# Three more products in the first down-projection round: eight plain block products in place of seven, and a new order of all work

## The chip, the cores and the metric

One core of one Trainium2 chip. The metric is the device time of one execution in microseconds (us), lower is better. The core has five engines that run side by side, each through its own list of instructions: PE multiplies matrices into PSUM, DVE (vector), ACT (scalar) and POOL (GpSimd) work elementwise, SP issues the DMA transfers.

## The reference, cut to what matters

```python
kv = einsum('bhsd,bhse->bhde', k, v); out = einsum('bhsd,bhde->bhse', q, kv)   # 4 x 8 heads, 576 tokens, 64
x = out / sqrt(mean(out*out, -1) + 1e-6) * g_norm       # -> x: 2304 tokens x 512
x = ((x @ w_a) * (x @ w_b)) @ w_out                     # first block, d_ff = 1536
return (sigmoid(x @ w_gate) * (x @ w_val)) @ w_out2     # second block, the same sizes
```

All of it is float32.

## The kernel before, in words

**Tiling.** The two blocks (m = 0, 1) are cut into six rounds each (q = 0 to 5); a round takes 256 of the 1536 middle columns (two weight chunks, u and v, of 128). In each round the 2304 tokens go in three groups (j = 0, 1, 2) of 768, each in two halves of 384. A group is named (m, q, j), and there are 36. Every matrix product is done by a Strassen scheme: the operands are cut into 2 x 2 blocks and seven block products replace eight, at the cost of sums and differences of blocks on the elementwise engines. A float32 operand is split into a high part, made by an ACT copy, and a low part, which is the source less the high part, made by DVE or POOL (h and l in names, lines 951 and 954 for activations, 536 and 540 for weights); a block product is three passes (high x high, high x low, low x high).

**A group's up-projection.** Seven products with u and v parts, 14 steps named `("P", g, i, "u" or "v")`, each of 6 matmuls of 384 columns (line 842). Then lines 899 to 919 form the product a*b: `gf1` (second half of the tokens) after products 5 and 4, `gf0` (first half) after product 3.

**A group's down-projection.** Seven products `("down", g, i)`, i from DOWNS = "1265734", each 6 matmuls (line 997). Their left operands are `G1` (the parts of `gf1`), and `S12`, `G22` and `S34`, which are the parts of sums of blocks made at line 934 (`s12g`, `s34g`). Their weights are four tiles `wo0` to `wo3`: `wo0` and half-tile `wo3` are parts of the weights, `wo1` and `wo2` are parts of block differences (`tmp`, line 520). Product 1 is common to two outputs: it opens PSUM pair 0, and `seed` (line 1004, ACT) copies it to pair 1. Pair 0 is held from product 1 to product 4. Results go into `part`: the first sum of an output block in round q = 0 is a plain copy (lines 447 and 449), all others are DVE additions (line 1026). So in round q = 0 a group has four copies and two additions.

**Weights.** They come as 64-bit words and are decoded on ACT, DVE and POOL (lines 475 to 497) into `w32`, then split by `w_parts` (line 512).

**What sets the order.** `Plan.order` (line 191) runs a list scheduler over all operations before the kernel is emitted: each has a cost, the operations it comes after, and a due time worked back from those that need it; an engine that comes free takes the ready operation with the least due time. `SHIFT` (line 57) adds a number of ns to the due time of a named operation: a positive one makes it less urgent. PSUM is four pairs of banks; pairs are given out strictly in the order in which the operations were created (line 259). Operations with `port=True` on DVE and POOL are never planned at the same time. The slots of line 41 say where the seven downs of the group before stand between the 14 product steps.

**Before the rounds.** The attention stage (lines 646 to 797) makes x in eighteen token tiles; its last tiles are still in work while the first two groups' products run. `x_comb` (line 553) makes the block sums of x of each group in round 0 (lines 567, 586, 589).

Of the kernel before, what the change touches and what calls it, by code (L numbers as in the profile page):

```python
# [46 lines left out]
DOWNS = "1265734"  # L47

# [17 lines left out]
    ('t13', 'wp', 1, 1): 170030, ('shift', (0, 'o')): 48280, ('clamp', (1, 'o')): 196670,  # L66
    ('t24', 'wo', (0, 0), 0): 67470, ('t13', 'wo', (0, 0), 1): 117760, ('wo0', (0, 0), 'l'): 59440,
# [16 lines left out]
    ('shift', (16, 'b')): 3400, ('t13', 'wp', 16, 0): 78700, ('wp0', 16, 'h'): 84360, ('wp3', 16, 'l'): 168520,
    ('t24', 'wp', 17, 1): -77400, ('clamp', (17, 'o')): 61540, ('wo3', (1, 2), 'h'): 70860, ('mag', (19, 'b')): 22720,
    ('w32', (19, 'b')): 35820, ('t13', 'wp', 18, 1): 5650, ('wo3', (1, 3), 'h'): 71380, ('load', (21, 'a')): -44050,
    ('shift', (21, 'a')): -34340, ('sign', (21, 'a')): -33010, ('last', (21, 'b')): 115060,
    ('t13', 'wp', 20, 0): 78700, ('wp2', 20, 'l'): 9920, ('t24', 'wp', 21, 0): -51740, ('t24', 'wp', 21, 1): -77490,
    ('mag', (21, 'o')): 180540, ('last', (22, 'b')): -23780, ('load', (23, 'a')): -49000, ('w32', (23, 'a')): -5650,
    ('t13', 'wp', 22, 0): 78700, ('wp2', 22, 'l'): 9920, ('t13', 'wp', 23, 0): -38040, ('xl', (0, 0, 0), '2'): 4130,  # L90
    ('xs', (0, 0, 0), '3'): -396300, ('P', (0, 0, 0), '2', 'u'): -414200, ('P', (0, 0, 0), '2', 'v'): -305030,
    ((0, 0, 0), 'c11'): 107780, ('P', (0, 0, 0), '7', 'v'): -29380, ('P', (0, 0, 0), '5', 'u'): 117720,
    ('P', (0, 0, 0), '5', 'v'): 49410, ((0, 0, 0), 'S12', 'l'): 186710, ((0, 0, 0), 'G22', 'h'): 162310,
    ((0, 0, 0), 'S34', 'l'): 92600, ('xh', (0, 0, 1), '2'): 42800, ('xl', (0, 0, 1), '2'): 119180,
    ('xh', (0, 0, 1), '7'): 269090, ('xh', (0, 0, 1), '4'): 21020, ('xl', (0, 0, 1), '4'): 27490,
    ('P', (0, 0, 1), '1', 'u'): 73740, ('P', (0, 0, 1), '1', 'v'): 88930, ('seed', (0, 0, 0)): 75880,
    ('P', (0, 0, 1), '5', 'u'): 98290, ((0, 0, 1), 'G22', 'l'): 39170, ((0, 0, 1), 'S34', 'h'): -72980,
    ('xs', (0, 0, 2), '5'): 154010, ('xl', (0, 0, 2), '7'): 15840, ('xl', (0, 0, 2), '4'): 30900,
    ('xs', (0, 0, 2), '3'): 335000, ('xl', (0, 0, 2), '3'): 98720, ('xd', (0, 0, 2), '3'): 332700,
    ('down', (0, 0, 1), '1'): 24410, ('P', (0, 0, 2), '2', 'u'): -128360, ('P', (0, 0, 2), '2', 'v'): 105070,  # L100
    ('down', (0, 0, 1), '5'): 19000, ('P', (0, 0, 2), '5', 'v'): 128990, ('P', (0, 0, 2), '4', 'v'): 28600,
    ((0, 0, 2), 'G1', 'l'): 163880, ((0, 0, 2), 'S34', 'h'): 74750, ('xh', (0, 1, 0), '6'): 60660,
    ('xh', (0, 1, 0), '3'): 193920, ('down', (0, 0, 2), '7'): 92580, ('sum', (0, 0, 2), '7'): 15470,
    ((0, 1, 0), 'S34', 'h'): -27040, ('down', (0, 1, 0), '2'): -197540, ('P', (0, 1, 1), '2', 'u'): -28400,
    ('down', (0, 1, 0), '6'): -86130, ('P', (0, 1, 1), '7', 'u'): -51550, ('down', (0, 1, 0), '5'): -33610,
    ('down', (0, 1, 0), '7'): -158610, ('down', (0, 1, 0), '3'): 20750, ('P', (0, 1, 1), '3', 'u'): 17430,
    ('P', (0, 1, 1), '3', 'v'): 139830, ('P', (0, 1, 2), '1', 'open'): 173480, ('P', (0, 1, 2), '2', 'v'): 5780,
    ('sum', (0, 1, 1), '5'): 31510, ('P', (0, 1, 2), '5', 'v'): -86130, ('P', (0, 2, 0), '5', 'open'): 13280,
    ('P', (0, 2, 0), '4', 'u'): 63490, ('P', (0, 2, 0), '4', 'v'): 144740, ('P', (0, 2, 1), '6', 'v'): -125580,
    ('P', (0, 2, 1), '2', 'v'): 17500, ('sum', (0, 2, 0), '5'): 24550, ('P', (0, 2, 1), '4', 'u'): 16740,  # L110
    ('P', (0, 2, 1), '4', 'v'): 8560, ('down', (0, 2, 0), '4'): 14790, ('P', (0, 2, 1), '3', 'u'): 17430,
    ('P', (0, 2, 1), '3', 'v'): 139830, ('P', (0, 2, 2), '1', 'open'): 139930, ('P', (0, 2, 2), '2', 'v'): 5780,
    ('P', (0, 2, 2), '5', 'v'): -86130, ('sum', (0, 2, 2), '6'): 186670, ('down', (0, 2, 2), '3'): 200070,
    ('P', (0, 3, 0), '4', 'v'): 144740, ('P', (0, 3, 1), '6', 'u'): -94550, ('P', (0, 3, 1), '6', 'v'): -125580,
    ('down', (0, 3, 0), '2'): -204820, ('P', (0, 3, 1), '2', 'u'): -28400, ('P', (0, 3, 1), '2', 'v'): 17500,
    ('P', (0, 3, 1), '5', 'u'): -60900, ('P', (0, 3, 1), '4', 'u'): 16740, ('P', (0, 3, 1), '4', 'v'): 8560,
    ('down', (0, 3, 0), '4'): 14790, ('P', (0, 3, 1), '3', 'u'): 17430, ('P', (0, 3, 1), '3', 'v'): 139830,
    ('P', (0, 3, 2), '1', 'open'): 139930, ('P', (0, 3, 2), '5', 'v'): -86130, ('P', (0, 3, 2), '3', 'u'): 1010,
    ('P', (0, 3, 2), '3', 'v'): -320, ('P', (0, 4, 0), '5', 'open'): 13280, ('down', (0, 3, 2), '3'): 200070,
    ('P', (0, 4, 0), '4', 'u'): 63490, ('P', (0, 4, 0), '4', 'v'): 144740, ('P', (0, 4, 1), '6', 'v'): -125580,  # L120
    ('P', (0, 4, 1), '2', 'v'): 17500, ('P', (0, 4, 1), '5', 'u'): -60900, ('P', (0, 4, 1), '5', 'v'): -27020,
    ('P', (0, 4, 1), '4', 'u'): 16740, ('P', (0, 4, 1), '4', 'v'): 8560, ('down', (0, 4, 0), '4'): 14790,
    ('P', (0, 4, 1), '3', 'u'): 17430, ('P', (0, 4, 1), '3', 'v'): 139830, ('P', (0, 4, 2), '3', 'u'): 1010,
    ('P', (0, 4, 2), '3', 'v'): -320, ('P', (0, 5, 0), '5', 'open'): 13280, ('down', (0, 4, 2), '3'): 200070,
    ('P', (0, 5, 0), '4', 'u'): 63490, ('P', (0, 5, 0), '4', 'v'): 144740, ('down', (0, 5, 0), '2'): -204820,
    ('P', (0, 5, 1), '2', 'v'): 17500, ('P', (0, 5, 1), '4', 'u'): 16740, ('P', (0, 5, 1), '4', 'v'): 8560,
    ('down', (0, 5, 0), '4'): 14790, ('P', (0, 5, 1), '3', 'u'): 17720, ('P', (0, 5, 1), '3', 'v'): 139070,
    ('P', (0, 5, 2), '1', 'open'): 140220, ('down', (0, 5, 2), '3'): 200070, ('sum', (0, 5, 2), '3'): 37620,
    ('xl', (1, 0, 2), '7'): -34020, ('xh', (1, 1, 0), '3'): 213490, ((1, 1, 0), 'c11'): -175520,
    ('P', (1, 1, 0), '5', 'u'): 123560, ((1, 1, 0), 'G1', 'l'): 39790, ((1, 1, 0), 'S34', 'h'): 35780,  # L130
    ('P', (1, 1, 1), '1', 'open'): 198010, ('P', (1, 1, 1), '7', 'u'): -21180, ((1, 1, 1), 'gf1'): 75540,
# [1006 lines left out]
```

## Time and profile before

| | us |
|---|---|
| median of 3 runs (lowest to highest) | 908.66 (908.51 to 909.37) |
| the profiled execution | 905.58 |
| its span, first to last instruction | 903.6 |
| PE busy | 861.3 (95%) |
| DVE busy | 728.9 (81%) |
| POOL busy | 476.7 (53%) |
| ACT busy | 463.5 (51%) |

The span is what the trace covers; the execution is 1.98 us longer. Busy shares are means over stages that differ: the table by stage, among the rows below, is what to read. In it "(x12)" counts instructions that start in the stage, and PEclk is the granted clock of TensorE, 1.00 for 2.4 GHz and 0.50 for 1.2 GHz. In a timeline the square brackets hold the idle time of the engine just before the instruction and what ended it.

### The profile page before, as it was taken

The numbers are of one execution on the slowest core, as the hardware profiler recorded it, in microseconds if no ns is written. First come the engines' busy times: TensorE is split into PE (matmuls) and PEld (weight loads), VectorE is DVE, ScalarE is ACT, GpSimd is POOL, SyncE is SP. The second block draws the span as 40 slices with busy tenths as digits, with TensorE's granted clock in tenths as the row PEclk, the third lists the DMA queues.
The fourth block names the chain that finished last, engine by engine and source line by source line (L and its number), as shares of the span: only waits on it lengthen the run. The fifth ranks groups of instructions, "written<-read, shape, count | busy, mean of one in ns | idle before, by whom it ended". The sixth has DMA issues, their size and how long they took to land.

```text
span 903.6 us, 13534 instructions
## 1 busy us (share of the span) xinstructions
PE 861.3 (95%) x4936; PEld 841.9 (93%) x4936; DVE 728.9 (81%) x995; ACT 463.5 (51%) x714; POOL 476.7 (53%) x411
## 2 busy tenths in 40 slices
PE   7788699999999999999999999999999999999997
PEld 6677599999999999999999989999999999999996
DVE  3778888878888888888889897887989888777666
ACT  3548566644445544544536566665556545434432
POOL 1547355456576647526548866465665636613202
PEclk9999899999999999999999999999999999999999
DMA  8896468899888888887865477988888888776763
GB/s 313 303 347 247 175 223 331 313 353 329 286 306 291 314 311 293 305 330 275 290 258 218 167 293 267 387 328 302 301 309 330 305 297 316 255 267 235 262 208 124
DMA packets 55026, 256.74 MB, mean 284 GB/s; under 512 B 6064, under 2 KB 9136, under 8 KB 54960
## 3 DMA queue, kind: packets, MB, share of 16 engines
q1 hardware_dynamic: 54960, 255.88, 77.6%
q8 instruction: 39, 0.64, 0.3%
q14 instruction: 27, 0.22, 0.1%
HBM read 218.10 MB, written 37.75 MB: 283 GB/s over the span
## 4 chain that ended last, share of the span: by engine, by line
PE 80%; DVE 7%; DMA 6%; ACT 3%; issue 2%; POOL 1%; SPq 0%; ACTq 0%; DVEq 0%
PE pair L842 50%; PE pair L997 26%; DMA raw<-w_all_dram 3%; PE pair L673 2%; DMA part<-kv_in_dram 2%; PE pair L745 1%; DVE pair L919 1%; DVE gf L899 1%; DVE G L954 1%; DMA x<-area 1%; DMA area<-kv_in_dram 1%; DVE part L1026 1%; PE pair L781 1%; DVE area L589 1%; DVE pair L899 0%
## 5 line engine op out<-in xcount | busy, mean ns | idle before, releaser
L842 PE MATMUL pair<-area,wp 128*128 128x384 f32 x3024 | 565.1, 339 | 7.5 <-DVE area L589 2.9
L842 PEld LDWEIGHTS pair<-area,wp 128*128 128x128 f32 x3024 | 532.0, 188 | 13.3 <-ACT pair L881 5.3
L1026 DVE TENSOR_TENSOR part<-pair,part 128x768 f32<-128x768 f32 x192 | 182.6, 954 | 43.9 <-PE pair L997 38.4
L997 PE MATMUL pair<-S,wo 128*128 128x384 f32 x864 | 167.2, 337 | 0.2 <-DVE part L1026 0.2
L497 POOL TENSOR_TENSOR w<-mag,last 128x512 int32<-128x512 int32 x72 | 96.9, 1351 | 110.3 <-DVE mag L491 108.4
L997 PEld LDWEIGHTS pair<-S,wo 128*128 128x128 f32 x864 | 152.5, 189 | 0.6 <-DVE part L1026 0.6
L997 PE MATMUL pair<-G,wo 128*128 128x384 f32 x648 | 132.0, 339 | 8.9 <-DVE gf L899 5.1
L997 PEld LDWEIGHTS pair<-G,wo 128*128 128x128 f32 x648 | 112.9, 188 | 15.2 <-issue 5.8
L934 POOL TENSOR_TENSOR s12g<-gf 128x384 f32<-128x384 f32 x28 | 30.6, 1091 | 86.6 <-DVE gf L899 86.4
L475 ACT ACTIVATE mag<-raw 128x512 f32<-128x512 f32 x72 | 47.8, 667 | 52.2 <-DMA raw<-w_all_dram 45.6
L951 ACT ACTIVATE G<-pair 128x768 fp32r<-128x768 f32 x36 | 29.0, 806 | 53.1 <-DVE pair L899 53.1
L536 ACT ACTIVATE wp<-tmp 128x512 fp32r<-128x512 f32 x48 | 29.8, 627 | 47.5 <-PE pair L842 26.3
L540 POOL TENSOR_TENSOR wp<-w,wp 128x256 fp32r<-128x256 f32 (+1 forms) x40 | 40.5, 1013 | 25.1 <-ACT wp L536 19.7
L540 POOL TENSOR_TENSOR wp<-tmp,wp 128x512 fp32r<-128x512 f32 x28 | 38.4, 1371 | 28.6 <-ACT wp L536 28.6
L491 DVE SCALAR_TENSOR_TENSOR mag<-raw,mag 128x512 uint32<-128x512 uint32 x72 | 52.3, 731 | 0.5
L479 ACT ACTIVATE last<-raw 128x512 int32<-128x512 uint32 x72 | 47.2, 661 | 8.8 <-DMA raw<-w_all_dram 8.8
L912 DVE TENSOR_TENSOR c<-pair,c 128x768 f32<-128x768 f32 x36 | 34.4, 955 | 20.2 <-PE pair L842 19.8
L483 DVE TENSOR_SCALAR mag<-mag 128x512 f32<-128x512 f32 x72 | 36.9, 521 | 17.0 <-ACT mag L475 17.0
L520 POOL TENSOR_TENSOR tmp<-w,tmp 128x256 f32<-128x256 f32 x53 | 42.5, 801 | 13.5 <-DVE tmp L520 6.1
L540 POOL TENSOR_TENSOR wo<-tmp,wo 128x512 fp32r<-128x512 f32 x19 | 24.6, 1293 | 39.1 <-ACT wo L536 32.8
L919 DVE TENSOR_TENSOR pair<-pair,u 128x768 f32<-128x768 f32 x36 | 34.6, 961 | 8.4 <-PE pair L842 8.1
L881 ACT ACTIVATE pair<-pair 128x768 f32<-128x768 f32 x36 | 28.7, 796 | 23.8 <-PE pair L842 20.7
(96 smaller groups left out, 1066.1 us busy)
## 6 DMA issues: line engine op xcount, KB each, us to landing
area<-x SPq DMA_DIRECT2D x210, 768.0 KB, 5.7
raw<-w_all_dram SPq DMA_DIRECT2D x72, 512.0 KB, 5.6
x<-area SPq DMA_DIRECT2D x42, 768.0 KB, 3.7
part<-kv_in_dram SPq DMA_DIRECT2D x12, 640.0 KB, 6.5
out_dram<-part SPq DMA_DIRECT2D x12, 384.0 KB, 2.4
area<-q_t_dram SPq DMA_DIRECT2D x15, 256.0 KB, 4.3
area<-kv_in_dram SPq DMA_DIRECT2D x4, 640.0 KB, 8.6
part<-q_t_dram SPq DMA_DIRECT2D x3, 256.0 KB, 10.3
```

The lines of the kernel that those rows point to most:

```text
L475: A.activation(out=tl["mag", k], in_=words(1).bitcast(F32), func=ACTF.Abs, scale=65536.0)
L479: A.activation(out=tl["last", k], in_=words(0), func=ACTF.Copy, scale=2.0**-29)
L483: V.tensor_scalar(out=m, in0=m, scalar1=LEAST, scalar2=MOST, op0=ALU.max, op1=ALU.min)
L491: V.scalar_tensor_tensor(out=m, in0=words(1), scalar=0x80000000, in1=m, op0=ALU.bitwise_and, op1=ALU.bitwise_or,)
L497: G.tensor_tensor(out=tl["w32", k].bitcast(I32), in0=tl["mag", k].bitcast(I32), in1=tl["last", k], op=ALU.add)
L520: eng.tensor_tensor(out=tl[name][:, cut], in0=tl[x[0]][:, x[1]], in1=tl[y[0]][:, y[1]], op=ALU.subtract)
L540: eng.tensor_tensor(out=t[:, 1, :], in0=tl[src][:, cut], in1=t[:, 0, :], op=ALU.subtract)
L842: nc.tensor.matmul(out=o, lhsT=wt[:, a, c], rhs=x[:, b, k, :], start=opens and k == 0 and (a, b) == (0, 0), stop=k == 1 and (a, b) == ab[- ...
L912: V.tensor_tensor(out=unit("c22"), in0=o(1), in1=unit("c22"), op=ALU.add)
L919: op((g, "c12"), "DVE", dve(n), lambda: V.tensor_tensor(out=o(), in0=o(), in1=tl[g, "u2"], op=ALU.add), done + [(g, "u2")], uses=[bank, (g ...
L997: nc.tensor.matmul(out=tl[bank][:, d], lhsT=tl[w][:, a, c], rhs=tl[x][:, e, half], start=opens and (a, e) == ab[0], stop=(a, e) == ab[-1], ...
L1026: V.tensor_tensor(out=acc, in0=tl[bank], in1=acc, op=ALU.add)
```

## The change

In the groups (0, 0, 0), (0, 0, 1) and (0, 0, 2) alone, the down-projection becomes eight plain block products, "a" to "h". They need two weight tiles (`wo0`, `wo1`: the parts of the two chunks as they are) and two activation tiles (`G1` from `gf1`, `S12` now the parts of `gf0`). Four PSUM pairs are used in turn, each by two products, after which it is copied to `part`. No sums (`s12g`, `s34g`), no `G22`, `S34`, no `seed`, no additions at line 1026 in those groups, and no differences for the weights of that round. The other 17 rounds go on with seven products.

The numbers in `SHIFT` are new for nearly all work of the rounds from (0, 1) on. Those of the front (attention, weight chunks 0 to 3, x and the products of (0, 0, 0) to (0, 0, 2)) are as they were, but for names that are gone and a few that go with them: `seed`, `S34`, `G22`, `down`, `t13`, `t24`.

```diff
+PLAIN, PLAINS = {(0, 0)}, "abcdefgh"
...
-    ('t24', 'wo', (0, 0), 0): 67470, ('t13', 'wo', (0, 0), 1): 117760, ('wo0', (0, 0), 'l'): 59440,
+    ('t13', 'wp', 1, 1): 170030, ('shift', (0, 'o')): 48280, ('clamp', (1, 'o')): 196670, ('wo0', (0, 0), 'l'): 59440,
     ('wo1', (0, 0), 'l'): 220590, ('clamp', (2, 'a')): 205050, ('shift', (2, 'b')): -43870, ('last', (3, 'a')): 77880,
...
-    ('P', (0, 0, 0), '5', 'v'): 49410, ((0, 0, 0), 'S12', 'l'): 186710, ((0, 0, 0), 'G22', 'h'): 162310,
-    ((0, 0, 0), 'S34', 'l'): 92600, ('xh', (0, 0, 1), '2'): 42800, ('xl', (0, 0, 1), '2'): 119180,
+    ('P', (0, 0, 0), '5', 'u'): 117720, ('P', (0, 0, 0), '5', 'v'): 49410, ((0, 0, 0), 'S12', 'l'): 186710,
...
+        for name, cut, x, y in () if kind == "wo" and F in PLAIN else differences:
...
         parts(0, whole, slice(0, 512), 512)
+        if kind == "wo" and F in PLAIN:
+            parts(1, half[0], slice(0, 512), 512)
+            return
...
         parts("G1", "gf1", (0, 1), [(g, "gf1")])
+        if g[:2] in PLAIN:
+            parts("S12", "gf0", (0, 1), [(g, "gf0")])
+            return
...
+    for n, (t, d) in enumerate(((1, 0), (1, 2), (0, 0), (0, 2))):
+        for half in range(2):
+            DOWN[PLAINS[2 * n + half]] = (("wo1", "wo0")[half], d // 2, ("S12", "G1")[t], half, 3 + n, (t, d))
...
-        opens = i in "15"
-        same = [k for k in DOWNS[:DOWNS.index(i)] if DOWN[k][4] == b]
+        plain, order = g[:2] in PLAIN, downs(g)
+        same = [k for k in order[:order.index(i)] if DOWN[k][4] == b]
+        opens = not same and b != 1
...
-        if same:
+        if plain and same:
+            before.append(("down", g, same[-1]))
+        elif same:
...
-        if to is None:
+        if to is None or plain and not same:
             return
...
+        for i in todo:
+            down(prev, i, at)
+            at += MMS
```

In `DOWN` an entry is: weight tile, its half, left operand, its half (u or v), PSUM pair, and the output block (token half, columns). The slots hold seven downs, so the eighth is created behind the next group's last product, with a due time to match.

## Rows read from the trace of the kernel before

**Rows 1.** The page, busy time of PE: us (share of span) and instructions.
```profile
PE 861.3 (95%) x4936; PEld 841.9 (93%) x4936; DVE 728.9 (81%) x995; ACT 463.5 (51%) x714; POOL 476.7 (53%) x411
```

**Rows 2.** Windows by stage: length, then busy us of each engine, clock, DMA.
```profile
84.40:109.80 25.40, 15.52 (x92) 12.66 (x90) 22.05 (x41) 17.77 (x29) 11.98 (x11) 0.97 0.47 184
109.80:126.00 16.20, 16.15 (x77) 15.83 (x77) 13.54 (x18) 10.42 (x15) 5.60 (x5) 0.83 0.74 271
126.00:200.00 74.00, 71.77 (x405) 70.46 (x406) 60.20 (x85) 41.91 (x64) 39.85 (x36) 1.00 0.81 305
200.00:470.00 270.00, 267.33 (x1517) 264.43 (x1516) 227.45 (x313) 127.85 (x200) 152.57 (x134) 1.00 0.84 302
470.00:600.00 130.00, 125.58 (x710) 123.00 (x709) 112.53 (x136) 79.01 (x116) 91.02 (x65) 1.00 0.69 267
600.00:875.00 275.00, 274.59 (x1564) 272.59 (x1563) 220.20 (x290) 135.38 (x205) 132.37 (x116) 1.00 0.82 290
875.00:903.60 28.60, 23.03 (x126) 21.49 (x124) 18.77 (x22) 7.20 (x10) 5.75 (x4) 1.00 0.30 111
```

**Rows 3.** Timeline of PE, 85 to 122 us: the downs of (0,0,0), one stalled product.
```profile
85.23 1.31 PE L997 MATMUL pair<-G,wo 128*128 128x384 f32 x6 [0.60 <-DVE gf L899]
...
90.59 1.31 PE L997 MATMUL pair<-G,wo 128*128 128x384 f32 x6 [1.16 <-ACT pair L1004]
...
109.77 3.89 PE L842 MATMUL pair<-area,wp 128*128 128x384 f32 x11 [2.46 <-DVE area L589]
113.45 3.05 PE L997 MATMUL pair<-S,wo 128*128 128x384 f32 x12
...
117.39 2.26 PE L997 MATMUL pair<-S,wo 128*128 128x384 f32 x12
...
120.54 1.22 PE L997 MATMUL pair<-G,wo 128*128 128x384 f32 x6
```

**Rows 4.** The chain of waits in order of time: start, us, what; same stretch.
```profile
109.77 3.89 PE pair L842 x11
113.66 2.85 PE pair L997 x12
...
117.55 2.10 PE pair L997 x12
```

**Rows 5.** Windows of 2.5 us about the stall at 109.8 us.
```profile
105.00:107.50 2.50, 1.46 (x9) 0.99 (x9) 2.33 (x4) 1.56 (x3) 0.00 (x0) 1.00 0.49 197
107.50:110.00 2.50, 0.23 (x1) 0.24 (x2) 2.12 (x4) 0.35 (x1) 0.00 (x0) 0.68 0.77 315
110.00:112.50 2.50, 2.50 (x9) 2.50 (x10) 2.50 (x5) 1.48 (x2) 0.00 (x0) 0.50 0.77 315
```

**Rows 6.** Timelines of DVE, POOL and ACT, 88 to 113 us: late parts.
```profile
110.83 0.95 DVE L954 TENSOR_TENSOR S<-s12g,S 128x768 fp32r<-128x768 f32 x1
111.70 0.68 DVE L540 TENSOR_TENSOR wo<-tmp,wo 128x512 fp32r<-128x512 f32 x1
...
94.47 0.99 POOL L954 TENSOR_TENSOR G<-gf,G 128x384 fp32r<-128x384 f32 x1
...
98.52 1.87 POOL L954 TENSOR_TENSOR S<-s34g,S 128x768 fp32r<-128x768 f32 x1
...
88.27 0.84 ACT L951 ACTIVATE S<-s12g 128x768 fp32r<-128x768 f32 x1
```

**Rows 7.** Waits of PE, 126 to 200 us: total us, times, longest.
```profile
PE pair L997 <- ACT pair L1004: 1.2, 1, 1.2
PE pair L842 <- ACT pair L881: 0.9, 1, 0.9
```

**Rows 8.** Groups by line and shape: busy us, mean ns | idle before.
```profile
L1026 DVE TENSOR_TENSOR part<-pair,part 128x768 f32<-128x768 f32 x192 | 182.6, 954 | 43.9 <-PE pair L997 38.4
...
L954 DVE TENSOR_TENSOR S<-s34g,S 128x768 fp32r<-128x768 f32 x17 | 19.5, 1147 | 6.0 <-ACT S L951 5.8
...
L934 DVE TENSOR_TENSOR s34g<-pair,s12g 128x384 f32<-128x384 f32 x36 | 19.9, 553 | 0.9
```

More of the change, by code (lines that the diff above doesn't have):

```diff
@@ L521, in difference @@
             return fn
-        for name, cut, x, y in (
-            (t13, c0, w12, w11), (t24, c0, w22, (t13, c0)), (t13, c1, w22, w12), (t24, c1, w21, (t24, c0)),
-        ):
+        differences = ((t13, c0, w12, w11), (t24, c0, w22, (t13, c0)), (t13, c1, w22, w12), (t24, c1, w21, (t24, c0)))
+        for name, cut, x, y in () if kind == "wo" and F in PLAIN else differences:
             first = cut is c0
@@ L971, in attention_then_two_moes, with downs, last_sum @@
             "4": ("wo2", 1, "G22", 0, 0, (0, 0))}
-    def last_sums(m, j):
-        g, found = (m, NQ - 1, j), {}
-        for i in DOWNS:
-            to = DOWN[i][5]
-            if to is not None:
-                found[to] = ("sum", g, i)
-        return found
+    for n, (t, d) in enumerate(((1, 0), (1, 2), (0, 0), (0, 2))):
+        for half in range(2):
+            DOWN[PLAINS[2 * n + half]] = (("wo1", "wo0")[half], d // 2, ("S12", "G1")[t], half, 3 + n, (t, d))
+    def downs(g):
+        return PLAINS if g[:2] in PLAIN else DOWNS
+    def last_sum(g, to):
+        return ("sum", g, [i for i in downs(g) if DOWN[i][5] == to][-1])
     def down(g, i, due):
@@ L1018, in down @@
         acc = rows(j, t)[:, d:d + 2]
-        earlier = [k for k in DOWNS[:DOWNS.index(i)] if DOWN[k][5] == to]
+        earlier = [] if plain else [k for k in order[:order.index(i)] if DOWN[k][5] == to]
         opening = q == 0 and not earlier
@@ L1030, in down @@
         elif q:
-            after = [("sum", (m, q - 1, j), [k for k in DOWNS if DOWN[k][5] == to][-1])]
+            after = [last_sum((m, q - 1, j), to)]
         else:
@@ L1035, in down @@
            uses=[bank], due=due + 2000)
-        if m == 1 and q == NQ - 1 and last_sums(m, j)[to] == ("sum", g, i):
+        if m == 1 and q == NQ - 1 and last_sum(g, to) == ("sum", g, i):
             t0 = (2 * j + t) * N
@@ L1073, in attention_then_two_moes @@
             else:
-                sums = last_sums(0, j)
-                x_ready[g, i] = x_comb(g, i, [sums[z] for z in quarters[i]])
-        todo = list(DOWNS) if prev else []
+                x_ready[g, i] = x_comb(g, i, [last_sum((0, NQ - 1, j), z) for z in quarters[i]])
+        todo = list(downs(prev)) if prev else []
         for slot in SLOTS if n < len(groups) - 1 else SLOTS_END:
@@ L1084, in attention_then_two_moes @@
                 at += MMS
+        for i in todo:
+            down(prev, i, at)
+            at += MMS
         prev = g
-    for i in DOWNS:
+    for i in downs(prev):
         down(prev, i, at)
```

299 rows, old and new, of the table SHIFT are left out of this document.

## The prediction

> **What bounds the kernel now.** I read the page's busy times first: PE is busy 95% of the span [rows 1]. That is a mean, so the table by stage comes next [rows 2]. From 200 to 875 us PE stands idle for only 2.67 + 4.42 + 0.41 = 7.5 us in 675 (stage length less PE busy, three rows): there PE is the bound, a product added costs its full length and a faster helper gains next to nothing. At the end (875 to 903.6) 5.57 us are idle, most of it after the last matmul. The stage to look at is 84.4 to 109.8 us: PE is busy 15.52 of 25.40, so 9.88 us are holes, while DVE is busy 22.05. Here the elementwise engines lead: the last attention tiles, the x sums of groups (0,0,1) and (0,0,2), weights being decoded, and the sums and parts of group (0,0,0) share them. From 109.8 to 126 PE is busy 16.15 of 16.20, but at a mean clock of 0.83.
>
> The timeline of PE says what stands where [rows 3]. Of the seven downs of (0,0,0), two run in the holes (85.23, 90.59). The other five (12 + 12 + 6 matmuls of line 997 at 113.45, 117.39 and 120.54) run behind the point at which PE is never again short of work for long. They are so late because their operands are: the low part of `S12` starts at 110.83 and that of a difference tile `wo` at 111.70 on DVE, and POOL makes `G22` and `S34` at 94.47 and 98.52 [rows 6]. SHIFT made these less urgent (186,710 ns for `S12` low, 220,590 for `wo1` low). The stall of 2.46 us before 109.77 is followed by work at half rate.
>
> **The change part by part.** I sum against the profiled execution, 905.58 us (span 903.6 and 1.98 around it). The median of the runs is 908.66, 3.08 more, so the sum's difference is put on 908.66.
>
> (a) Three products are added, one per group. Twelve matmuls of line 997 at full clock advance the chain by 2.10 us [rows 4], so six take 1.05, and three products 3.15 if nothing hides them. For groups (0,0,1) and (0,0,2), whose downs run in the stage 126 to 200 with 2.23 us idle in 74 [rows 2], nothing does: +2.10.
>
> (b) Group (0,0,0) is another matter. Its products a to d need `G1`, whose use opened at 85.23 [rows 3], and the two plain weight tiles; e to h need the parts of `gf0`, with no `s12g` sums before them. Gone from the queue of work that is not urgent are four weight differences, two weight parts, four sums, `G22` and `S34`: at 94.47 and 98.52 POOL has slots of 0.99 and 1.87 us that fall free [rows 6]. `S12` low and `wo1` low keep their SHIFT but have little left to be put behind. So I expect them before 100 us and six of the eight products in the holes, two behind, where five stood: 3 x 1.05 = -3.15. The bounds: all eight in the holes, -5.25; only two, as now, and six behind, +1.05. A hole is at most 2.46 us and a product 1.05, so a product put there can delay an attention step; that is why I don't take eight.
>
> (c) The stall and the slow stretch. The wait is 2.46 us. After it 11 matmuls took 3.89 and 12 took 2.85 us where 12 take 2.10 [rows 4]: 23 x 0.175 = 4.03, so 2.71 were lost; the granted clock was 0.50 there, 1.2 GHz, after a stretch with PE busy 0.23 of 2.50 us [rows 5]. What PE waited for is a DVE low part of x at the end of the attention chain. DVE loses in 84 to 110 us three sums of 0.553 [rows 8] and a weight part of 0.68 [rows 6]: 2.3 us of 22.05. The pair that product 1 holds until product 4, 85 to 121 us, is now free after two products, which lets product 5 of (0,0,1) open earlier and gives PE other work. I take half of 2.46 + 2.71: -2.6 (bounds: 0 and -5.2).
>
> By the Trainium skill, "TensorE: Matmul & The Clock Gate", part 1, an idle PE is put to half rate and activity releases it. The trace agrees (0.50 after the stall, 1.00 before it in spite of shorter holes). The rule also speaks against the change: products spent early in the holes are no longer there to cover the stall itself, and if it stays, so does the slow clock; then (c) would be 0 and the sum 2.6 us higher.
>
> (d) Helpers in 110 to 200 us. Per group two additions (0.954 each), three sums (0.553) and one part (1.147) leave DVE: 4.7 us [rows 8], and one ACT copy goes. The copies of four output blocks stay. PE's waits there that this can shorten are 1.2 us on the downs' `seed` and 0.9 on the products' [rows 7], of 2.23 idle. Half: -1.1 (bounds 0 and -2.2). In the changed groups the first of the two waits has no cause any more, but the one seen at 199.45 may belong to the round after. What is late next is the x of (0,0,2), seven low parts on DVE and POOL.
>
> (e) The new order from (0,1) on and at the end. It removes no work; it can win at most the 7.5 us of idle time from 200 to 875 and little at the end, and it can lose on waits that a planner's costs don't hold. 4.42 of the 7.5 lie in 470 to 600, between the blocks. I take 0, between -4.4 (that stretch made tight) and +5 (17 rounds, each 0.3 worse).
>
> Code, transfers and SP's queue: the same number of loads and stores, fewer instructions; nothing.
>
> Sum: 2.10 - 3.15 - 2.6 - 1.1 + 0 = -4.75: 900.8 in a profiled execution, 908.66 - 4.75 = 903.9 as a median.
>
> **The rivals.**
>
> R1, the better one: all eight products in the holes, the clock stays up, and PE is led by its own work from 85 us: 2.10 - 5.25 - 5.2 - 1.1 = -9.45, 899.2. For it: holes of 9.88 us hold 8.4 us of products. Against it: the x of (0,0,2) hangs on the last attention tile, and seven low parts of it follow.
>
> R2, no change: `S12` low stays late because its due time keeps the 186,710. Then a to d alone are in the holes and four behind instead of five: 2.10 - 1.05 - 1.1, and (c) is 0: -0.05, 908.6. For it: it ran at 110.83 though its ACT half started at 88.27 [rows 6]. Against: the competition it lost to is mostly gone.
>
> R3, slower: `wo1` low is late. It keeps 220,590, and product a, which opens the first of the four PSUM pairs, needs it; pairs are given out in a fixed order, so b to h and product 5 of (0,0,1) stand behind a. If it stays at 111.7 us [rows 6], no down fills a hole and eight instead of five stand behind: 3 x 1.05 + 2.10 = 5.25, less 1.1 of (d): +4.15, 912.8. It decides from where more than five of the eight are behind. Against it: in the old kernel that tile was a difference with two late steps before it; now it needs one decoded chunk.
>
> R4, also slower: the new order of the steady rounds. If one in two of the 17 remaining rounds gains a wait like the 1.2 us on the `seed` [rows 7], that is +9.6, and with the rest -4.75: +4.85, 913.5. It takes four such waits to undo the forecast. For it: three stages run with nearly no idle time now (0.41 us in 275), so a reorder can only spoil them.
>
> **How the numbers follow.** Chances: forecast 0.50, R1 0.12, R2 0.13, R3 0.10, R4 0.15. Forecast and R1 are faster by over 0.2% (1.8 us, about what a measurement of this kernel can tell from no change) but for 0.04; R2 is mostly no change; R3 and R4 slower but for 0.02. So faster 0.60, same 0.17, slower 0.23. The range is 898.0 to 913.0: it leaves out the far part of R1 and of R4, some 0.18 in all. The likeliest case alone, with the bounds of (b) to (d) halved, is 901 to 907.
>
> **What would show it.** (a) 4936 + 18 = 4954 matmuls. (b) In the changed kernel's timeline of PE, downs of (0,0,0) between 84 and 108 us: six by forecast, four by R2, none by R3; low parts of `S12` and `wo` before 100 us. (c) PE holes in that stage near 4 us instead of 9.88, and a granted clock above 0.9 from 108 to 116. (d) No wait on line 1004's successor before 200 us. (e) 7.5 us, give or take 2, of PE idle from 200 to the last stage. Wrong it is if PE is as idle before 126 us as now, or if idle time after 200 us grows by more than 4.75.

## The result and the profile after

The changed kernel took 898.97 us (median of six runs, 896.82 to 900.25) beside 908.59 (906.99 to 911.16) for the kernel before on the same chip: a ratio of 0.9892 [0.9872, 0.9911], 9.6 us faster. A second set of six gave 899.03 and 0.9893 [0.9859, 0.9926]. The prediction said 903.9: the sign was right and the size half of what came. Rival R1 had 899.2.

One thing about the base comes first. The kernel before was profiled four times in all, at 905.58, 908.16, 910.54 and 908.48 us (mean 908.2); its largest set, 29 runs, lies between 904.89 and 911.76. The profile that the prediction was summed against is thus 2.6 us under the mean. The changed kernel's three profiles took 900.25, 899.93 and 899.51 (mean 899.9); its 12 runs lie between 895.35 and 902.10, so it spreads about as much as the kernel before. Profile against profile the change is worth 8.3 us, and a pair of single profiles shows as little as 5.3.

The page of the changed kernel (us, share of the span, instructions) answers to [rows 1]: 18 more matmuls, fewer instructions on the other engines.

```profile
PE 860.7 (96%) x4954; PEld 841.9 (94%) x4954; DVE 724.8 (81%) x986; ACT 451.1 (50%) x693; POOL 464.2 (52%) x400
```

The table by stage of the changed kernel, with the columns of [rows 2]; its span is 898.4.

```profile
84.40:109.80 25.40, 23.33 (x146) 21.88 (x144) 21.82 (x38) 15.37 (x25) 12.06 (x10) 1.00 0.51 200
109.80:126.00 16.20, 13.86 (x78) 12.67 (x76) 14.95 (x18) 10.82 (x17) 7.38 (x7) 1.00 0.33 130
126.00:200.00 74.00, 73.03 (x413) 71.53 (x413) 58.23 (x84) 35.75 (x55) 34.56 (x29) 1.00 0.94 356
200.00:470.00 270.00, 266.77 (x1512) 263.73 (x1511) 231.45 (x310) 124.72 (x194) 154.15 (x135) 1.00 0.83 298
470.00:600.00 130.00, 125.83 (x709) 123.11 (x708) 111.03 (x138) 79.84 (x118) 87.77 (x65) 1.00 0.70 273
600.00:875.00 275.00, 274.77 (x1570) 273.28 (x1569) 217.50 (x289) 135.63 (x205) 125.09 (x112) 1.00 0.79 285
875.00:898.40 23.40, 17.81 (x96) 16.27 (x95) 16.25 (x19) 4.62 (x6) 5.75 (x4) 0.94 0.35 131
```

Between 84.4 and 109.8 us PE starts 146 matmuls where it started 92, and its holes shrink from 9.88 to 2.07 us. The next stage has 2.34 us of holes that were not there, but the clock is 1.00 in it instead of 0.83. The timeline of PE of the changed kernel shows what fills the holes (start, us, engine, line, idle before in brackets; line 1129 has the downs, 969 the up-projection's products, which the text calls products, 908 the transposes of attention). It answers to [rows 3].

```profile
86.10 2.52 PE L1129 MATMUL pair<-G,wo 128*128 128x384 f32 x12
88.45 2.26 PE L969 MATMUL pair<-area,wp 128*128 128x384 f32 x12
90.55 2.25 PE L1129 MATMUL pair<-G,wo 128*128 128x384 f32 x12
94.67 0.63 PE L908 MATMUL pair<-ident,area 128*128 128x128 f32 x4 [1.87 <-ACT part L572]
...
104.08 1.21 PE L1129 MATMUL pair<-S,wo 128*128 128x384 f32 x6
...
105.48 1.28 PE L1129 MATMUL pair<-S,wo 128*128 128x384 f32 x6
...
108.68 1.31 PE L1129 MATMUL pair<-S,wo 128*128 128x384 f32 x6
110.49 0.66 PE L908 MATMUL pair<-ident,area 128*128 128x128 f32 x4 [0.50 <-DVE part L576]
110.90 1.29 PE L1129 MATMUL pair<-S,wo 128*128 128x384 f32 x6
```

Four of the eight downs of (0,0,0) run before 93 us, two between 104 and 107, and the last two stand just before and just behind the last transposes, at 108.68 and 110.90, while PE would else wait for the end of the attention chain. In the kernel before, five of seven stood behind that end. The longest wait of PE from 84 to 112 us is 1.87 us. The windows of the changed kernel about its longest hole and where the stall was, against [rows 5]:

```profile
92.50:95.00 2.50, 0.63 (x5) 0.36 (x4) 2.36 (x3) 2.01 (x3) 2.33 (x2) 1.00 0.69 285
...
105.00:107.50 2.50, 2.50 (x18) 2.46 (x17) 2.47 (x5) 1.39 (x2) 1.51 (x1) 1.00 0.16 49
107.50:110.00 2.50, 2.47 (x16) 1.87 (x14) 1.63 (x3) 1.15 (x3) 1.27 (x2) 1.00 0.45 175
110.00:112.50 2.50, 2.01 (x13) 2.01 (x14) 1.71 (x3) 1.25 (x3) 1.47 (x2) 1.00 0.55 202
```

The granted clock stays at 1.00 in all four. In each of the four profiles of the kernel before it fell to 0.50 at least once between 95 and 120 us; in the three of the changed kernel it did not. The operands were ready earlier. In the timelines of DVE and POOL, against [rows 6], the low parts of the round's two weight tiles start at 74.60 and 85.30, and `S12` low at 101.00 (it was 110.83), 1 us past the 100 that the prediction named.

```profile
74.60 0.68 DVE L664 TENSOR_TENSOR wo<-w,wo 128x512 fp32r<-128x512 f32 x1
...
101.00 0.95 DVE L1081 TENSOR_TENSOR S<-gf,S 128x768 fp32r<-128x768 f32 x1
...
85.30 1.29 POOL L664 TENSOR_TENSOR wo<-w,wo 128x512 fp32r<-128x512 f32 x1
```

The chain of waits of the changed kernel (start, us, what) has the downs there at full clock, 1.04 us for six matmuls where 2.85 went by for twelve [rows 4]:

```profile
104.24 1.04 PE pair L1129 x6
```

The waits of PE in the changed kernel from 126 to 200 us (total us, times, longest), against [rows 7]: the wait on `seed` is not there, and a transfer of x has come in. (In the third profile of the changed kernel there is a wait of 1.4 us on `seed`; below it turns out not to belong to the edited groups.)

```profile
PE pair L969 <- DMA area<-x: 0.6, 1, 0.6
PE pair L1129 <- DVE gf L1026: 0.3, 1, 0.3
```

The groups by line and shape show what left DVE, against [rows 8]: six additions of 0.95 us and three of each of the sums.

```profile
L1160 DVE TENSOR_TENSOR part<-pair,part 128x768 f32<-128x768 f32 x186 | 176.7, 955 | 41.7 <-PE pair L1129 34.2 <-ACT wo L660 1.9 <-ACT last L604 0.3
...
L1061 DVE TENSOR_TENSOR s34g<-pair,s12g 128x384 f32<-128x384 f32 x33 | 18.3, 555 | 0.9
```

**Where the time went.** PE does the groups in one order, each with 84 matmuls of the product line, so the start of every 84th such matmul is a mark that can be found in any trace by counting. It is called here after the group that it opens; a group's first products can overlap the last of the group before, so it may lie a few matmuls beside that group's own first one. The table gives the marks for each kernel in us against the mean of the four profiles of the kernel before; a minus is earlier. Each column but the first two is one profile, and they come from three chips (medians of the kernel before there: 907.08 to 908.39). The kernels with plain downs have more downs behind them at a mark: at (0,0,2) 8 for 7, at (0,1,2) 31 for 28.

| mark | before, mean (largest deviation) | changed, mean (spread) | plain_old_order | seven_new_order | behind8 | old_sums | old_sums_12 | plain2_searched |
|---|---|---|---|---|---|---|---|---|
| (0,0,1) | 81.6 (±0.9) | +1.1 (-0.1 to +1.8) | +0.5 | -0.4 | -0.7 | -0.6 | -1.9 | -0.5 |
| (0,0,2) | 124.4 (±1.4) | -9.2 (-10.8 to -8.1) | -9.4 | +0.6 | -1.6 | -8.1 | -12.0 | -11.1 |
| (0,1,2) | 192.3 (±1.4) | -4.9 (-6.4 to -3.7) | -5.3 | +0.6 | +5.0 | +9.5 | -4.4 | -6.7 |
| (0,3,0) | 284.5 (±2.0) | -6.8 (-7.5 to -6.3) | -3.3 | +0.1 | +4.6 | +8.4 | +1.8 | -8.3 |
| (1,0,0) | 487.9 (±2.5) | -8.0 (-8.6 to -7.1) | -2.1 | -0.2 | +2.6 | +6.4 | -0.2 | -10.2 |
| (1,5,2) | 870.0 (±2.6) | -8.2 (-8.7 to -7.8) | -1.5 | +1.3 | +4.2 | +6.9 | +0.1 | -4.9 |
| profiled execution | 908.2 (±2.6) | -8.3 (-8.7 to -7.9) | -1.7 | +1.2 | +3.9 | +6.9 | +0.1 | -5.2 |

Read down the column of the changed kernel: the whole gain, and more, is made between (0,0,1) and (0,0,2); 4.3 us are given back by (0,1,2), of which 2.1 are the last two added products; and 3.4 come after that, 1.9 of them by (0,3,0).

### The profile page after: what moved, and what is told of

Same layout as the page of the kernel before. It is cut to its first block, busy times and chain, and to the rows that moved or that the text cites. A ratio compares the mean times of both kernels' runs of the same rounds, so it can differ in the third digit from the quotient of the medians.

```text
span 898.4 us, 13519 instructions
## 1 busy us (share of the span) xinstructions
PE 860.7 (96%) x4954; PEld 841.9 (94%) x4954; DVE 724.8 (81%) x986; ACT 451.1 (50%) x693; POOL 464.2 (52%) x400
## 4 chain that ended last, share of the span: by engine, by line
PE 73%; DVE 10%; DMA 9%; ACT 3%; issue 3%; POOL 2%; SPq 0%; ACTq 0%; POOLq 0%; DVEq 0%
PE pair L969 46%; PE pair L1129 25%; DMA raw<-w_all_dram 4%; DMA x<-area 2%; DVE part L1160 1%; PE pair L800 1%; DMA area<-x 1%; DVE pair L1046 1%; DVE gf L1026 1%; POOL area L716 1%; DVE G L1081 1%; PE pair L872 1%; DMA area<-kv_in_dram 1%; DMA part<-kv_in_dram 1%; DVE mag L616 1%
## 5 line engine op out<-in xcount | busy, mean ns | idle before, releaser
L1160 DVE TENSOR_TENSOR part<-pair,part 128x768 f32<-128x768 f32 x186 | 176.7, 955 | 41.7 <-PE pair L1129 34.2
L1129 PE MATMUL pair<-S,wo 128*128 128x384 f32 x864 | 169.3, 337 | 1.7 <-DVE gf L574 1.3
L1129 PE MATMUL pair<-G,wo 128*128 128x384 f32 x666 | 134.2, 338 | 5.4 <-DVE gf L1026 3.8
L1129 PEld LDWEIGHTS pair<-G,wo 128*128 128x128 f32 x666 | 115.9, 188 | 10.5 <-issue 6.0
L608 DVE TENSOR_SCALAR mag<-mag 128x512 f32<-128x512 f32 x72 | 34.9, 492 | 26.0 <-ACT mag L600 25.7
L716 POOL TENSOR_TENSOR area<-s,area 128x768 fp32r<-128x768 f32 x17 | 31.6, 1859 | 30.3 <-ACT area L713 30.3
L645 POOL TENSOR_TENSOR tmp<-w,tmp 128x256 f32<-128x256 f32 x48 | 37.3, 777 | 14.5 <-DVE wp L664 7.1
L1081 POOL TENSOR_TENSOR S<-s34g,S 128x768 fp32r<-128x768 f32 x18 | 34.3, 1903 | 15.3 <-ACT S L1078 12.0
```

Of the source, the lines that this page charges most:

```text
L645: eng.tensor_tensor(out=tl[name][:, cut], in0=tl[x[0]][:, x[1]], in1=tl[y[0]][:, y[1]], op=ALU.subtract)
L716: eng.tensor_tensor(out=tl[xin][:, 1], in0=source(), in1=tl[xin][:, 0], op=ALU.subtract)
L1081: eng.tensor_tensor(out=tl[name][:, 1], in0=tl[g, src][:, cut], in1=tl[name][:, 0], op=ALU.subtract)
L1129: nc.tensor.matmul(out=tl[bank][:, d], lhsT=tl[w][:, a, c], rhs=tl[x][:, e, half], start=opens and (a, e) == ab[0], stop=(a, e) == ab[-1], ...
L1160: V.tensor_tensor(out=acc, in0=tl[bank], in1=acc, op=ALU.add)
```

## The experiments

Two explanations stood against each other. Theory A: the front alone, eight plain products in the holes. Theory B: the order of the 11 other rounds. (There are 12 rounds, two blocks of six. Where the part above speaks of 17 others, and an expectation below of 18 in all, the count is wrong.)

**The same two kernels again: how large is the noise?** No edit.

> The kernel before as it is, for a second profile. The first profiled execution, 905.58 us, is near the fast end of 904.9 to 911.8; its granted clock was 0.50 for 6.8 us behind the stall at 107 to 110 us. If the spread of this kernel comes from the front (transfers, the stall and how long the slow clock lasts), a profile near 908 shows 2 to 3 us more idle time or slow clock before 126 us and the same stages, within 1 us, from 200 us on.

> The changed kernel as it is, on the same chip as the others and with a second profile. Median 898 to 900 and ratio 0.988 to 0.991 by both theories. The first profiled execution (900.25) was the slowest of six, with a start 1.84 us later than before's; if that is the spread of the first 80 us alone, this profile shows the same idle time as the first from 84 us on, within 1 us.

> The kernel before, a third profile, to place the part of the gain that the profiled executions do not show: they stand 5.3 to 8.2 us apart, the medians 9.6. If it lies in the front of the kernel before (the start, the stall at 107 to 110 us, how long the slow clock lasts), the time at which the last product of (0,0,1) ends varies here by 2 us or more and the rest follows it. If it lies in the rounds, the front agrees within 1 us and the idle time from 200 to 470 us varies, which was 2.7 us in the first profile and 4.3 in the second.

> The kernel before, a fourth profile, for the same question and with the same two expectations as the third.

> The changed kernel, a third profile. The first two, 900.25 and 899.93, are 1 us above its median of 899.0. By both expectations no slow clock between 84 and 126 us and the first product of (0,0,2) between 114 and 117 us; the rest within 1.5 us of the first two.

Measured: 908.16, 910.54 and 908.48 us for the kernel before, profiled; 899.93 and 899.51 for the changed one, 899.03 the median of its second set. Its third profile comes to (0,0,2) at 113.58 us, 0.4 before the range that was expected. The gain stands, and a single profile of the kernel before can be 2.6 us off. Neither place that the expectations name has the spread alone: the four profiles lie within 2.5 us of each other at (0,0,2) and within 5.0 at the end, and PE's idle time from 200 to 470 us is 2.67, 4.31, 4.68 and 3.38 us. Part of it is the clock. Three windows of the third profile of the kernel before show a slow stretch from 95 us, behind waits of no more than 1.62 us, and a second at 112.5, at the end of the long stall:

```profile
95.00:97.50 2.50, 0.91 (x4) 0.91 (x5) 2.36 (x7) 1.85 (x3) 1.01 (x2) 0.62 0.00 0
97.50:100.00 2.50, 2.50 (x14) 2.50 (x14) 0.78 (x1) 0.00 (x0) 2.42 (x2) 0.50 0.92 378
...
112.50:115.00 2.50, 2.37 (x7) 2.38 (x8) 2.50 (x5) 1.47 (x2) 0.00 (x0) 0.54 0.66 275
```

**Theory A alone: eight plain products, all other numbers of SHIFT as before.**

```diff
 PLAIN, PLAINS = {(0, 0)}, "abcdefgh"
-SHIFT = the changed kernel's
+SHIFT = that of the kernel before, entire
```

> The changed kernel's eight plain products in the groups (0,0,0) to (0,0,2), with the SHIFT numbers of the kernel before (those of names that are gone have no effect). Theory A, the holes: nearly all of the gain of 9.6 us is the front, where the eight products of (0,0,0) fill PE's idle time from 84 to 112 us; then this kernel stands at 900 to 902 us, 0.990 to 0.993 of before. Theory B, the new order: the front gives what was forecast, 4.75, and the rest comes from the searched order of the other rounds; then it stands near 904, ratio 0.995.

Measured: 906.29, ratio 0.9981 [0.9955, 1.0006]; the profile 906.52. Neither theory had this time (900 to 902, or 904). The twelve runs lie far apart, from 901.25 to 911.35, so the one profile is a sample of them. In it the front gains as much as in the changed kernel (-9.4 us at (0,0,2)), and most of it is gone by (1,0,0). The waits of PE in this kernel from 126 to 350 us (line 1005 has the downs, 845 the products) say where:

```profile
PE pair L1005 <- DVE gf L902: 4.1, 4, 2.2
PE pair L1005 <- ACT pair L1012: 3.0, 1, 3.0
PE pair L845 <- DMA area<-x: 0.9, 1, 0.9
PE pair L845 <- ACT pair L884: 0.5, 2, 0.3
```

They are 8.5 us. The same view of the changed kernel has 3.3:

```profile
PE pair L1129 <- DVE gf L574: 1.3, 1, 1.3
PE pair L969 <- DVE part L1160: 0.9, 1, 0.9
PE pair L969 <- DMA area<-x: 0.6, 1, 0.6
PE pair L1129 <- DVE gf L1026: 0.5, 2, 0.3
```

The 3.0 us wait can be followed one step further in the timeline of ACT, first of plain_old_order, then of the kernel before, then of the changed kernel:

```profile
194.39 0.67 ACT L476 ACTIVATE mag<-raw 128x512 f32<-128x512 f32 x1 [3.95 <-DMA raw<-w_all_dram]
...
196.92 0.80 ACT L1012 ACTIVATE pair<-pair 128x768 f32<-128x768 f32 x1
```

```profile
197.31 0.66 ACT L475 ACTIVATE mag<-raw 128x512 f32<-128x512 f32 x1 [2.28 <-DMA raw<-w_all_dram]
...
198.61 0.79 ACT L1004 ACTIVATE pair<-pair 128x768 f32<-128x768 f32 x1
```

```profile
191.71 0.68 ACT L600 ACTIVATE mag<-raw 128x512 f32<-128x512 f32 x1 [0.41 <-DMA raw<-w_all_dram]
...
193.02 0.79 ACT L1136 ACTIVATE pair<-pair 128x768 f32<-128x768 f32 x1
```

In plain_old_order ACT sat 3.95 us on a decoding step of a weight whose transfer had not landed. `seed` (line 1012) stood behind it in ACT's fixed list, and PE waited for `seed`. A decoding step stands ahead of `seed` in the other two as well: in the kernel before, ACT waited 2.28 us for its transfer, and PE 1.2 us for `seed` [rows 7]. From the mark (0,1,2) to the decoding step are 5.8 to 7.1 us in the four profiles of the kernel before, 7.5 in plain_old_order and 3.9 to 6.0 in the three of the changed kernel. So under the old order PE came earlier and the transfer less so, and under the new order the transfer came earlier too, though not in every execution: in the third profile of the changed kernel ACT still waited 2.50 us and PE 1.4. All this lies behind the mark (0,1,2), where the downs are those of (0,1,1), so this `seed` belongs to a group that the edit leaves as it is.

**Theory B alone: seven products, the changed kernel's order.**

```diff
-PLAIN, PLAINS = {(0, 0)}, "abcdefgh"
+PLAIN, PLAINS = set(), "abcdefgh"
...
+    (the old numbers of the twelve names that only seven products have)
```

> Seven products in all 18 rounds, with the changed kernel's SHIFT numbers for all other work (the twelve front names that the change dropped have their old numbers). Theory A: the new order alone is worth little, 0 to 2 us: 907 to 909, ratio 0.998 to 1.000, and the stall with the slow clock at 107 to 115 us is there as in the kernel before. Theory B: some 5 us faster, ratio 0.9945.

Measured: 907.39, ratio 0.9997 [0.9978, 1.0015]. Theory B falls: with seven products the new order is worth nothing that can be told. Its profile stays within 1.3 us of the mean of the kernel before at every mark, and it has the slow clock too, from 94.8 and from 111.8 us.

**The eight products, but not in the holes.** All downs of (0,0,0) are made to wait for two late products of (0,0,1). Product 5 of (0,0,1), which takes its PSUM pair behind theirs, is held back with them.

```diff
+        if g == (0, 0, 0) and i in "abcdefgh":
+            before += [("P", (0, 0, 1), "2", "v"), ("P", (0, 0, 1), "7", "v")]
```

> The changed kernel with all eight products of group (0,0,0) held back until products 2 and 7 of (0,0,1) are done, so that few of them stand in the holes from 84 to 100 us; DVE, ACT and POOL keep all their relief. Theory A: the eight stand in PE's busy stretch instead, 8 x 1.05 = 8.4 us, less what they then fill of later waits: 905 to 908, ratio 0.996 to 0.999. Rival C, the relief of the helpers and not the place of the products: 899 to 902, ratio 0.990 to 0.993.

Measured: 911.8, ratio 1.0037 [1.0016, 1.0057]; the profile 912.11. Two rows of its timeline of PE show the old stall back, with the same length and the same releaser as in [rows 3], and the downs behind it; the windows show the clock:

```profile
106.29 3.89 PE L969 MATMUL pair<-area,wp 128*128 128x384 f32 x11 [2.47 <-DVE area L716]
109.97 4.61 PE L1129 MATMUL pair<-G,wo 128*128 128x384 f32 x24
```

```profile
102.50:105.00 2.50, 0.83 (x5) 0.58 (x5) 1.61 (x3) 1.13 (x2) 0.00 (x0) 0.75 0.51 214
105.00:107.50 2.50, 1.21 (x4) 1.21 (x5) 2.50 (x4) 0.31 (x1) 0.00 (x0) 0.50 0.44 179
107.50:110.00 2.50, 2.50 (x10) 2.50 (x9) 2.50 (x5) 0.53 (x1) 0.00 (x0) 0.50 0.58 236
```

Both theories missed the time (905 to 908 by theory A, 899 to 902 by rival C). At (0,0,2) it stands at -1.6 where the changed kernel has -9.2. So 7.6 us lie between these two kernels, which differ in where the downs and product 5 stand, the stall and its slow clock included. The 1.6 are not the worth of the rest of the edit: behind8 has eight downs behind the stall where the kernel before has five, 3.15 us more work there, and its stall still ends 3.5 us earlier (106.29 for 109.77). How much of that is the lighter load of the helpers, and how much that no down stands between the attention steps, was not tried apart. What stands in the holes matters to the attention chain. Its last transposes start here, and in the kernel before, at

```profile
103.00 0.66 PE L908 MATMUL pair<-ident,area 128*128 128x128 f32 x4 [0.78 <-ACT part L572]
```

```profile
106.47 0.66 PE L781 MATMUL pair<-ident,area 128*128 128x128 f32 x4 [0.78 <-ACT part L447]
```

and in the changed kernel at 110.49. Work put into the holes goes with a later end of the attention chain; it pays because PE is busy meanwhile.

**The old sums put back beside the plain products.** The sums and parts that the edit took from DVE, POOL and ACT are made again, their results unused, and product h waits for them; first in all three groups, then in (0,0,1) and (0,0,2) alone. The additions of line 1026 and the weight differences are not put back, and the sums that read `gf1` keep its PSUM pair longer.

```diff
+            sums("s12g", 0, ("gf0", 0), ("gf0", 1), ALU.add)
+            ...
+            parts("G22", "gf0", (1,), [(g, "gf0")])
+            parts("S34", "s34g", (0, 1), [(g, "s34g", "v")])
...
+        if plain and i == "h":       # old_sums_12: and g[2]
+            before += [(g, "G22", "l"), (g, "S34", "l")]
```

> The changed kernel, eight plain products, but the sums s12g and s34g and the parts G22 and S34 of the groups (0,0,0) to (0,0,2) are made again, used by nobody; product h waits for the parts as the old products did. That puts back 4 sums of 0.55 to 1.1 us and two low parts of 1.0 and 1.9 us per group on DVE and POOL and two ACT copies. Theory A, the place of the products: a to g still fill the holes, the stall stays away, and the front loses 1 to 3 us: 900 to 903, ratio 0.991 to 0.994. Theory C, the relief of the helpers makes the front: 906 to 909, ratio 0.997 to 1.000, with the first product of (0,0,2) back near 121 us.

> As old_sums, but the unused sums and parts are made for the groups (0,0,1) and (0,0,2) alone; group (0,0,0) is as in the changed kernel. The front up to the first product of (0,0,2) is then the changed kernel's. Theory E: what old_sums lost between 126 and 200 us it lost to the helpers' work for these two groups, which makes the weights of round (0,1) late: a stall behind an ACT part of a weight and 907 to 913, ratio 0.998 to 1.005. Theory F: the loss came from the front, where the sums of (0,0,0) moved everything after them: 900 to 904, ratio 0.991 to 0.995.

Measured: 913.11, 1.005 [1.0028, 1.0072], and 908.11, 1.0023 [1.0006, 1.004]. In old_sums, slower than both theories had it, the front still gains 8.1 us, against theory C, and then 17.6 are lost by (0,1,2). One row of its timeline of PE and one window tell most of it:

```profile
148.22 2.44 PE L971 MATMUL pair<-area,wp 128*128 128x384 f32 x6 [4.90 <-ACT wp L662]
```

```profile
126.00:200.00 74.00, 66.17 (x342) 64.43 (x341) 55.44 (x83) 36.03 (x57) 31.42 (x29) 0.91 0.84 314
```

A weight part of round (0,1) came 4.9 us late, and the clock fell with it (0.91 in the mean). In old_sums_12 the time is in theory E's range, but not by its mechanism: the front is even earlier (-12.0), (0,1,2) is level with the changed kernel, and the gain is lost between there and (0,3,0), behind the groups that were edited. Taken alone old_sums would say that the relief of the helpers matters for the next round's weights. But any edit of the front without a new order for it loses its gain later, as plain_old_order did, so what the relief itself is worth stays open.

**Is a search of the order alone enough?** The kernel before, its SHIFT changed at random, a change kept where the scheduler's own plan did not grow.

```diff
-SHIFT = that of the kernel before
+SHIFT = one found by that search
```

> The kernel before, seven products everywhere, with SHIFT numbers searched anew for some 40 minutes from its own: random changes, kept where the list scheduler's plan does not get longer. Rival D, the gain is one of searching, with seven products as with eight: 4 us faster or more, ratio under 0.996, with fewer holes from 84 to 110 us or less idle time after 200. Theory A: the stall behind the late operands of (0,0,0) cannot be ordered away, so at most 2 us, ratio 0.998 to 1.001.

Measured: 913.3 (six runs, 910.37 to 920.8), ratio 1.0063 [1.004, 1.0085]: slower, outside both expectations, though the plan was not longer. A plan is not the chip. This does not settle rival D for an order found with other means: seven products with an order fitted to them as the changed kernel's was to its eight were not tried.

**The same edit at the second block's first round.**

```diff
-PLAIN, PLAINS = {(0, 0)}, "abcdefgh"
+PLAIN, PLAINS = {(0, 0), (1, 0)}, "abcdefgh"
...
+    (numbers searched anew about those rounds)
```

> The changed kernel with eight plain products in the first round of the second block, (1,0), too, and SHIFT numbers of the rounds around it searched in the same way for 25 minutes. The changed kernel's PE is idle 4.2 us from 470 to 600, where the x sums of the second block fall. If theory A holds there as well, three products more (3.15 us) are hidden in part and 2 to 3 us of idle time go: 897 to 900, ratio 0.987 to 0.991, not clearly better than the changed kernel. If helpers there are not what PE waits for, 902, ratio 0.9925.

Measured: 902.91, 0.9965 [0.995, 0.9981]: faster than the kernel before, but with less gain than the changed one, and near the 902 that was expected if helpers are not what PE waits for there. Its windows from 470 us:

```profile
470.00:600.00 130.00, 127.22 (x714) 125.90 (x713) 102.76 (x131) 75.08 (x110) 69.74 (x51) 0.99 0.74 278
600.00:875.00 275.00, 272.88 (x1550) 269.67 (x1549) 218.45 (x287) 127.82 (x194) 121.24 (x101) 1.00 0.77 280
```

Idle time between the blocks falls from 4.17 to 2.78 us, which does not pay for three more products (3.15), and 600 to 875 gains 1.9 us of idle. Since the numbers about these rounds come from the search that made seven_searched slower, the products and the order are not told apart here. No version beat the changed kernel.

## Why the prediction was half right

The sign, the stage and the mechanism of the front were right. The step that failed is the size of the front, (b) and (c): half of the stall and its slow clock was taken and two products were left behind, -5.75 us, where the marks have -9.2. Two more terms, (d) and (e), were wrong and all but cancel each other:

| stretch | forecast | measured |
|---|---|---|
| to (0,0,2): (b) + (c) | -3.15 - 2.6 = -5.75 | -9.2 |
| (0,0,2) to (0,1,2): two products of (a), and (d) | 2.10 - 1.1 = +1.0 | +4.3 |
| (0,1,2) to the end: (e) | 0 | -3.4 |
| sum | -4.75 | -8.3 |

**(a) Three more products.** Right in the count, 4954 matmuls. At the price of 1.05 us each the two of the later groups are 2.1 of the 4.3 us given back.

**(b) Mis-sized.** The step was "six of the eight products in the holes, two behind". By the mark that the prediction set, six start by 108 us, as it said; but the other two were not behind. They ran beside the last transposes, by 112.2, in time that had been lost. So none is behind where five were: at 1.05 us each 5.25 us instead of 3.15. The fear that a product in a hole delays an attention step was right: the last transposes start at 110.49 where they started at 106.47 (2.4 us later in the means of the profiles, 1.1 of it there at the mark (0,0,1) already), and at 103.00 in behind8. It cost little, because 73 product matmuls behind the mark (0,0,1) ran before PE waited for the end of that chain (0.48 us, at 113.90), where 49 did in the kernel before (2.46 us).

**(c) Mis-sized.** Half of 2.46 + 2.71 was taken; the whole went, the stall and the slow clock, in three profiles of three. With (b) this is 5.25 + 5.17 = 10.42 us, and between (0,0,1) and (0,0,2) the traces have 10.2 in the mean. That was R1's front, taken at 0.12. The prediction's reason, that product 5 of (0,0,1) opens earlier and gives PE other work, agrees with these counts. The objection that products spent early would not be there to cover the stall failed: the stall's place is filled by products of (0,0,1) and the last two downs, and behind8, which keeps them for later as the objection would have it, has the stall back at 2.47 us. In the front of the changed kernel both are gone; which of the two carries how much of the 5.17 was not tried apart. A slow stretch does not need the long stall, as the third profile of the kernel before shows at 95 us.

**(d) Wrong sign.** The step was that fewer helpers' operations shorten PE's waits after 110 us, -1.1. The larger of its two waits, 1.2 us on `seed` at 199.45, was not the edited groups' at all: it is (0,1,1)'s and hangs on a weight's transfer, as the timelines of ACT above show. That it is missing from the changed kernel's first profile is no merit of (d). Instead 4.3 - 2.1 = 2.2 us were lost. Between the marks (0,0,2) and (0,1,2) PE is idle for 2.29 us where it was 1.02 (2.82 and 2.79 in the other two profiles). Of this 1.32 us are a wait on `G1` low, which DVE reached at 118.48, behind a weight difference that took 2.06 us:

```profile
116.16 2.06 DVE L645 TENSOR_TENSOR tmp<-w,w 128x256 f32<-128x256 f32 x1
118.48 0.94 DVE L1081 TENSOR_TENSOR G<-pair,G 128x768 fp32r<-128x768 f32 x1
```

The same shape took 0.42 us in the kernel before (at 109.63). In the changed kernel it took 2.06 or 2.07 us there in all three profiles, while POOL was at a sum of x (115.92 to 117.94 in this one); that the two held each other up is likely and not shown. Another 0.6 us are a transfer of x, in a stretch whose DMA share rises from 0.81 [rows 2] to 0.94. The rest of the 2.2 is not followed. The working looked at what the helpers lose and not at what PE, 9 us earlier, runs into.

**(e) Taken as nothing; it was needed.** The working asked what the new order could win from 7.5 us of idle time and found little. With seven products that is just what was measured (0.9997). But with eight, the old order loses the front's gain: from (0,1,2) to the end plain_old_order goes from -5.3 to -1.7, and the changed kernel from -4.9 to -8.3. So with eight products the order is worth 7 us there and nothing before (one profile against three; the medians, 906.29 and 899.03, say the same), and a sum of separate terms could not hold it. The medians agree: -1.7 us for the front alone (0.9981, which can't be told from no change), nothing for the order alone, -9.6 for both. The changed kernel's own idle time from 200 to 875 us is 7.63, as the forecast had it (7.5 give or take 2). The 3.4 us are in part the base's: the three other profiles of the kernel before lose 1.3 to 3.4 us between (0,1,2) and (1,5,2) against the first, in waits of PE and, in two of them, in a slow stretch after 190 us that the changed kernel's profiles have not. How its numbers were found stays open.

**The rivals.** R1 came out at its time (899.2 for 898.97) with its front right; that the rest agrees is luck, since the kernel lost 2.2 us where R1 had -1.1 and won 3.4 that R1 did not have. R2 and R3 fall with `S12` low at 101.00 and the weight parts at 74.60 and 85.30. R4 was not seen in the changed kernel; a loss of that kind happens to the front's gain under the old order. R4 and the far bound of (e) count 17 other rounds where there are 11: with one in two of 11, R4's 9.6 us would be 6.6 and its time 910.5, and the bound of +5 would be +3.3.

## What to carry to other kernels

The scheme with fewer products need not be the faster one where the matrix engine stands idle for its operands: in group (0,0,0) a plain scheme with more products and earlier operands cost nothing, and the clock stayed up as well; in the two groups behind it the added products are paid for, and at the second block's first round a first try did not pay. A gain in front of statically ordered rounds has to be carried through them: try the edit with the old order and with one fitted to it before it is judged, for neither alone was worth anything that could be told here. The base, too, should have an order fitted to it with the same effort, which was not done here. And read the kernel before several times if its runs spread by as much as the change is expected to bring.

## What was not expected of the hardware

A wait of 1.87 us, in a window where PE was busy 0.63 of 2.50 us, left the granted clock at 1.00; in the stall of 2.46 us, in one with 0.23 [rows 5], it fell to 0.50; and in the third profile of the kernel before it fell in a window with 0.91, where the longest wait was 1.62 us. So the longest single wait does not tell by itself whether the clock falls. A single core moved 356 GB/s at a DMA share of 0.94 for 74 us, and PE lost only 0.6 us there to a transfer (1.2 and 1.1 in the other two profiles). The kernel before spreads by 6.9 us over 29 runs, the changed one by 6.8 over 12. The four profiles of the kernel before have one, one, three and two stretches at 1.2 GHz between 80 us and the last matmuls, the three of the changed kernel none.
